# A two-stage expert kernel on one core: moving the first bytes of the streamed tiles from 96 to 48 mod 128

## The chip, the core and the metric

The kernel runs on one core of one Trainium2 chip. The metric is device time in microseconds (us) of one execution; three runs of the kernel before are given, and one further execution was profiled. The engines are TensorE (in the profile PE for matmuls, PEld for the loads of the stationary operand), VectorE (DVE), ScalarE (ACT), GpSimd (POOL) and SyncE (SP, which only issues DMAs here).

## What is computed

The reference takes 8 sequences of 3072 tokens with 256 features and runs three steps, all in float32 accuracy:

```python
X = np.fft.fft(np.fft.fft(x, axis=1), axis=2).real      # 8 x 3072 x 256
x = X.reshape(-1, 256)
h = x @ w_in                                             # 256 -> 2048
x = (h / (1 + np.exp(-1.702 * h))) @ w_out               # 2048 -> 256
e = argmax(x @ w_gate)                                   # of 8 experts, for rows with x @ w_skip > 0
out = x + gate * (relu(x @ w1[e]) @ w2[e])               # 256 -> 1024 -> 256; other rows: out = x
```

## The kernel before

**Numbers.** Every large product is made with operands in the format `fp32r`, each split in a high and a low part, and three matmuls take the place of one: high by high, low by high, high by low. A matmul streams the columns of one operand (the moving tile, 256 columns of 4 bytes in most of them) through 128 columns of the other (the stationary tile), which a LDWEIGHTS loads into the array ahead of it. So each matmul in this kernel has a load of its own, and each load runs beside the matmul before.

**Phase 1** is the class `Phase1`: 16 half-sequences of 768 columns, each in 3 blocks of 256 columns with 8 steps, 384 steps in all. The transform over the tokens is folded into small real matrices `cmat` (L262, 384 columns, 9 matmuls a piece, stationary tiles `sh` and `sl`); its result is written to `yh` and `yl` by ACT, DVE and POOL (`evac_even`, `evac_odd1`, L275 to L296). The transform over the features is folded into the first layer's weights, `wch` and `wcl`. Step g issues, in this order on PE: the first layer (`hstep`, L836, 12 matmuls: `yh` or `yl` streamed, `wch` or `wcl` stationary), then the second layer of step g-2 (`ystep`, L867, 24 matmuls of 264 columns: `woh` or `wol` streamed, `gh` or `gl` stationary), and between them now and then a piece of the next half-sequence's transform or a count for the routing (L779, L781). DVE, ACT and POOL turn a first layer's result into `gh` and `gl` meanwhile.

**Between the phases** (`last_block`) the first blocks of expert 0 are made with the tiles of phase 1: L1030 (`axh` and `axl` streamed, `w1h` and `w1l` stationary, 96 matmuls) and L1065 (`w2h` and `w2l` streamed, `ahh` and `ahl` stationary, 96 matmuls).

**Phase 2** is the class `Phase2`: for each expert, blocks of 256 rows, some of them in a loop whose number of turns comes from the data. A block is `first` (L1253, 48 matmuls: `xh` or `xl` streamed, `w1h` or `w1l` stationary) and `second` (L1289, 48 matmuls: `w2h` or `w2l` streamed, `hh` or `hl` stationary). The 41 blocks of this run give 1968 matmuls on either line. A block's rows are transposed and written to `xh` and `xl` at L1220 and L1221; the next expert's weights are split into `w1h` to `w2l` at L1203 and L1204.

**Where tiles start.** A tile lies at the same bytes of all 128 partitions. The allocator puts each at a multiple of 32 bytes, one after the other, so a small unused tile (`skew`) moves those behind it. In the built program before, the streamed tiles of L836, L1253, L1289 and L1065 start at byte 96 mod 128 and their stationary tiles at byte 32 mod 128. Slices of them lie a multiple of 128 bytes further on, so that this holds for each matmul.

Of the kernel before, what the change touches and what calls it, by code (L numbers as in the profile page):

```python
# [13 lines left out]
F32R = mybir.dt.float32r  # L14
# [9 lines left out]
P = 128  # L24
S = 3072
D = 256
FF = 2048
E = 8
F2 = 1024
# [3 lines left out]
HC = 768  # L33
PB = 256
# [121 lines left out]
def skew(pool, words):  # L156
    pool.tile([P, words], F32, name="skew")


class Phase1:  # L160
    def __init__(self, tc, ctx, nb, a, reg, k):
        self.tc, self.nc, self.nb, self.a, self.reg, self.k = tc, tc.nc, nb, a, reg, k
        self.ident, self.xs = k["ident"], k["xs"]
        self.side = defaultdict(list)
        self.pos = defaultdict(list)
        self.rts = {}
        self.scattered = False
        nc = self.nc
        cp = self.cp = ctx.enter_context(tc.tile_pool(name="cp", bufs=1))
        self.wch = cp.tile([P, 2, FF], F32R, name="wch")  # L170
        self.wcl = cp.tile([P, 2, FF], F32R, name="wcl")
        self.woh = cp.tile([P, NF, NW], F32R, name="woh")
        self.wol = cp.tile([P, NF, NW], F32R, name="wol")
        self.w128 = cp.tile([P, NF], F32, name="w128")
        self.coef = cp.tile([P, 2, CW], F32, name="coef")
        self.spec = cp.tile([P, 4, nb], F32, name="spec")
        self.mini = cp.tile([P, 8], F32, name="mini")
        self.tri = cp.tile([P, 2, P], BF16, name="tri")
        self.rid = cp.tile([P, 2, 4, 2], F32, name="rid")
        self.k8 = cp.tile([P, 4, 8], F32, name="k8")  # L180
        self.base = cp.tile([P, 8], F32, name="base")
        self.base0 = cp.tile([P, 8], F32, name="base0")
        dp = self.dp = ctx.enter_context(tc.tile_pool(name="dp", bufs=1, space=DRAM))
        self.yd = dp.tile([nb, 2, HC], F32, name="yd")
        self.ydm = dp.tile([nb, 1], F32, name="ydm")
        self.ps = ctx.enter_context(tc.tile_pool(name="ps", bufs=1, space=PSUM))
        self.left = ctx.enter_context(ExitStack())
        self.right = ctx.enter_context(ExitStack())
        self.yr = self.open(self.right, "yr", "right")
        self.fa = self.open(self.right, "fa", "right")  # L190
# [105 lines left out]
        le.tensor_sub(dl, xt, dh)  # L296

    def new_y(self, hb):
        pool = self.yl if hb % 2 else self.yr
        return [pool.tile([P, 2, HC], F32R, tag=t, name=t) for t in ("yh", "yl")]  # L300

    def new_s(self):
        sh = self.fa.tile([P, 4, 3, P], F32R, tag="sh", bufs=1, name="sh")
# [30 lines left out]
    def startup(self):  # L334
        nc, a, tc, nb = self.nc, self.a, self.tc, self.nb
        ps = self.ps
        v, act, pool = nc.vector, nc.scalar, nc.gpsimd
# [238 lines left out]
        def close():  # L576
            sts.close()
            self.yl = self.open(self.left, "yl")
            skew(self.yl, 24)
            self.rp = self.open(self.left, "rp")  # L580
            self.fb = self.open(self.right, "fb", "right")
            self.fbufs = 1
# [62 lines left out]
        at(3, "b", load_c, 5)  # L645
        at(4, "b", load_c, 4)
        at(9, "a", close)
        self.cm = cm

# [482 lines left out]
class Phase2:  # L1132
# [25 lines left out]
    def tiles(self):  # L1158
        tc, ctx = self.tc, self.ctx
        cp = self.cp = ctx.enter_context(tc.tile_pool(name="cp2", bufs=1, side="right", reuse_waits="tile"))  # L1160
        self.sp = ctx.enter_context(tc.tile_pool(name="sp2", bufs=2, side="right", reuse_waits="tile"))
        self.xh = cp.tile([P, 2, PB], F32R, name="xh")
        self.xl = cp.tile([P, 2, PB], F32R, name="xl")
        self.cur = cp.tile([P, 2, RW], F32, name="cur")
        skew(cp, 24)
        self.turns, self.t = {}, {}


# [6 lines left out]
    def top(self, e, v=None):  # L1175
        self.t[e] = self.load((self.turns[e] if v is None else v) * PB + e * self.reg, "top", "top")
# [10 lines left out]
        self.r[e] = r1, r2  # L1187

    def weights(self, e):
        shapes = (("w1h", [P, 2, F2]), ("w1l", [P, 2, F2]), ("w2h", [P, E, D]), ("w2l", [P, E, D]))  # L1190
        pool = self.wp[e % 2]
        self.w[e] = [pool.tile(s, F32R, tag=t, name=t) for t, s in shapes[:2]]
        if e < 2:
            skew(pool, 16)
        self.w[e] += [pool.tile(s, F32R, tag=t, name=t) for t, s in shapes[2:]]

    def split(self, e, i):
        r, w = self.r[e], self.w[e]
# [97 lines left out]
    def run(self):  # L1296
        nc, tc = self.nc, self.tc
        self.pool(1)
        self.ps = self.ctx.enter_context(tc.tile_pool(name="ps2", bufs=1, space=PSUM, reuse_waits="tile"))
        hp = self.ctx.enter_context(tc.tile_pool(name="hp2", bufs=1, reuse_waits="tile"))  # L1300
        skew(hp, 16)
        self.hh, self.hl = (hp.tile([P, E, PB], F32R, name=n) for n in ("hh", "hl"))
        w, t, turns, top = self.w, self.t, self.turns, self.top
        top(1)
        self.raws(1, nc.scalar)
        kw = {} if self.sync == "barrier" else dict(iteration_sync=self.sync)
        for e in range(E):
            more = e + 1 < E
            if more and e:
                top(e + 1)  # L1310
            with tc.For_i(0, turns[e], 1, **kw) as i:  # L1311
                nx = self.load(((turns[e] if e else self.v0) - i - 1) * PB + e * self.reg, "nx")
                s, ix = self.first(w[e], {1: self.ready})
                tc.stage_boundary()
                self.transpose(nx)
                self.second(w[e], s, ix, nx, {(0, 2): self.ready, (0, 3): tc.stage_boundary, (0, 5): self.ready, (0, 7): tc.stage_boundary, (1, 4): self.ready})
            if more:
                self.weights(e + 1)

            def mid():  # L1320
                tc.epilogue_barrier()
                if more:
                    tc.prologue_barrier()

            s, ix = self.first(w[e], {j: (lambda j=j: [self.split(e + 1, 2 * j - 2 + z) for z in range(2)]) for j in range(1, 4)} if more else {}, mid)
            if more:
                self.transpose(t[e + 1])
                self.split(e + 1, 6)
                self.split(e + 1, 7)
            if e + 2 < E:  # L1330
                if self.pads is not None:
                    self.pads(e + 2)
                self.raws(e + 2)
            self.second(w[e], s, ix, None)
            if more:
                nc.vector.tensor_copy(self.cur, t[e + 1])
# [49 lines left out]
```

## Time and profile before

| | |
|---|---|
| median of 3 runs | 2401.2 us (2398.43 to 2401.38) |
| profiled execution, its own time | 2397.02 us |
| its span, first to last instruction | 2394.9 us |
| mean granted TensorE clock | 0.997 of 2.4 GHz |
| PE busy | 2341.7 us (98%), 19222 matmuls |
| DVE, ACT, POOL busy | 1652.3 us (69%), 1121.5 us (47%), 1399.2 us (58%) |
| matmuls of L867, L836, L1253, L1289 | 9216, 4608, 1968, 1968 |

The share of a busy PE counts each matmul from its start to a modelled end some 280 ns later, while the next one starts 113 to 125 ns after it. So neither the share nor the mean duration of one matmul tells how fast they follow each other; the start times in the timeline do.

### The profile page before, as it was taken

To read this page: it belongs to the slowest core of one execution; us is meant where nothing else is said; L and a number is where in the kernel's file an instruction comes from. 1 tells how busy PE (TensorE), PEld (TensorE's weight loads), DVE (VectorE), ACT (ScalarE), POOL (GpSimd) and SP (SyncE) were. 2 spreads that over 40 slices of the span, in tenths; PEclk is the share of its full clock that TensorE was granted. 3 is DMA by queue.
4 is the path that set the end of the run, shared out by engine and by line. 5 is a ranking of instruction groups with operands and counts; after the bars stand their busy time and mean duration, and the time that the engine had idled before them with its cause. 6 is when DMAs were issued, how large, how long until landed. Compare 5 with 4: busy or idle time off the path is not lost. (4 is left out here: it accounts for less than half of the span.)

```text
span 2394.9 us, 50491 instructions
## 1 busy us (share of the span) xinstructions
PE 2341.7 (98%) x19222; PEld 2310.1 (96%) x19222; DVE 1652.3 (69%) x3429; ACT 1121.5 (47%) x1451; POOL 1399.2 (58%) x868
## 2 busy tenths in 40 slices
PE   5999999999999999999999999999999999999999
PEld 4899999999999999999999999999999999999999
DVE  7679679767966886697679668965757445555543
ACT  5544545454554554545445544544545333433332
POOL 3567667676677776777767767667666312323211
PEclk9999999999999999999999999999999999999999
DMA  7302311231222113112312221130101312323111
GB/s 263 116 34 78 126 44 66 69 100 41 66 94 68 48 65 118 47 38 86 115 35 79 71 90 48 59 107 21 61 21 33 108 45 85 117 85 119 37 44 40
DMA packets 91450, 178.82 MB, mean 75 GB/s; under 512 B 10896, under 2 KB 66751, under 8 KB 85105
## 3 DMA queue, kind: packets, MB, share of 16 engines
q1 hardware_dynamic: 69488, 96.12, 13.0%
q0 software_dynamic: 20448, 77.87, 9.4%
q8 instruction: 132, 2.16, 0.4%
q10 hardware_dynamic: 1312, 2.10, 0.3%
q14 instruction: 70, 0.57, 0.1%
HBM read 126.21 MB, written 66.59 MB: 81 GB/s over the span
## 5 line engine op out<-in xcount | busy, mean ns | idle before, releaser
L852 POOL TENSOR_TENSOR gl<-h,gh 128x1024 fp32r<-128x1024 f32 x384 | 924.5, 2408 | 510.6 <-ACT h L851 441.9
L850 ACT ACTIVATE gh<-h 128x1024 fp32r<-128x1024 f32 x384 | 407.6, 1061 | 848.1 <-DVE h L843 700.3
L867 PE MATMUL py<-woh,gh 128*128 128x264 f32 x3072 | 773.0, 285 | 2.1 <-ACT rows L873 1.5
L867 PE MATMUL py<-wol,gh 128*128 128x264 f32 x3072 | 770.5, 284 | 0.0
L867 PEld LDWEIGHTS py<-woh,gh 128*128 128x128 f32 x3072 | 578.8, 188 | 4.2 <-ACT rows L873 3.8
L867 PEld LDWEIGHTS py<-wol,gh 128*128 128x128 f32 x3072 | 579.9, 189 | 0.0
L840 DVE SCALAR_TENSOR_TENSOR pp<-rb,w,pt 128x256 f32<-128x256 f32 x768 | 333.3, 475 | 323.0 <-PE pt L836 322.4
L867 PE MATMUL py<-woh,gl 128*128 128x264 f32 x3072 | 459.7, 284 | 0.8 <-POOL gl L852 0.8
L836 PE MATMUL pt<-yh,wch 128*128 128x256 f32 x1536 | 434.3, 283 | 3.2 <-DVE pp L840 2.4
L836 PE MATMUL pt<-yh,wcl 128*128 128x256 f32 x1536 | 429.5, 280 | 1.9 <-DVE wcl L431 1.9
L836 PE MATMUL pt<-yl,wch 128*128 128x256 f32 x1536 | 429.5, 280 | 0.6 <-POOL yl L296 0.4
L851 ACT ACTIVATE h<-h 128x1024 f32<-128x1024 f32 x384 | 407.5, 1061 | 36.2 <-ACT gh L850 1.5
L867 PEld LDWEIGHTS py<-woh,gl 128*128 128x128 f32 x3072 | 408.5, 188 | 1.0 <-POOL gl L852 1.0
L842 DVE TENSOR_TENSOR h<-pp,pt 128x512 f32<-128x512 f32 x384 | 263.9, 687 | 52.7 <-POOL gl L852 1.7
L836 PEld LDWEIGHTS pt<-yh,wch 128*128 128x128 f32 x1536 | 290.9, 189 | 4.4 <-DVE pp L840 3.0
L836 PEld LDWEIGHTS pt<-yl,wch 128*128 128x128 f32 x1536 | 291.1, 190 | 1.0 <-POOL yl L296 0.6
L836 PEld LDWEIGHTS pt<-yh,wcl 128*128 128x128 f32 x1536 | 289.6, 189 | 2.1 <-DVE wcl L431 2.1
L1267 POOL DMA_INDIRECT out<-ob,ix x82 | 80.6, 983 | 338.3 <-DVE ob L1281 336.1
L843 DVE TENSOR_TENSOR h<-pp,pt 128x512 f32<-128x512 f32 x384 | 261.1, 680 | 0.0
L799 POOL DMA_INDIRECT xs<-rows,rix x192 | 194.3, 1012 | 44.0 <-issue 26.0
L1289 PE MATMUL po<-w2h,hh 128*128 128x256 f32 x656 | 189.3, 289 | 0.0
L1253 PE MATMUL h<-xh,w1h 128*128 128x256 f32 x656 | 183.6, 280 | 5.2 <-PEq L1311 4.1
(221 smaller groups left out, 3456.3 us busy)
## 6 DMA issues: line engine op xcount, KB each, us to landing
cmat<-cm POOLq DMA_DIRECT2D x48, 1158.0 KB, 5.6
raw<-raw SPq DMA_DIRECT2D x48, 512.0 KB, 4.8
out<-rows SPq DMA_DIRECT2D x48, 512.0 KB, 2.9
r<-w SPq DMA_DIRECT2D x14, 1024.0 KB, 6.6
nx<-xs SPq DMA_DIRECT2D x33, 266.0 KB, 3.0
rb<-yd SPq DMA_DIRECT2D x48, 128.0 KB, 3.1
wide<-w_in SPq DMA_DIRECT2D x8, 512.0 KB, 8.7
wide<-w_out SPq DMA_DIRECT2D x8, 512.0 KB, 6.1
```

The lines of the kernel that those rows point to most:

```text
L799: i = self.nc.gpsimd.indirect_dma_start(self.xs, bass.IndirectOffsetOnAxis(ap=ix[:, t : t + 1], axis=0), rows[:, t], None, bounds_check=E ...
L836: nc.tensor.matmul(pt[z][:, i], lhsT=w_[:, z, f], rhs=x_[:, z, cols], start=n == 0, stop=n == 2)
L840: v.scalar_tensor_tensor(pp[:, i], r, self.w128[:, 2 * s + i : 2 * s + i + 1], pt[0][:, i], ALU.mult, ALU.add)
L842: v.tensor_add(h[:, :, 0], pp, pt[1])
L843: v.tensor_sub(h[:, :, 1], pp, pt[1])
L850: nc.scalar.activation(gh, hv, AF.Gelu_apprx_sigmoid)
L851: nc.scalar.activation(hv, hv, AF.Gelu_apprx_sigmoid)
L852: nc.gpsimd.tensor_sub(gl, hv, gh)
L867: nc.tensor.matmul(ys[gb][t], lhsT=x_[:, i, tk], rhs=w_[:, 2 * s + i], start=s == 0 and part is hi and n == 0, stop=ends and part is lo an ...
L1253: nc.tensor.matmul(h[:, z], lhsT=w_[:, k, f * P : (f + 1) * P], rhs=x_[:, k], start=i == 0, stop=i == 5)
L1267: d = self.nc.gpsimd.indirect_dma_start(self.out, bass.IndirectOffsetOnAxis(ap=ix, axis=0), ob, None, bounds_check=self.ntok - 1, oob_is_e ...
L1289: self.nc.tensor.matmul(po[t], lhsT=x_[:, f, t * P : (t + 1) * P], rhs=w_[:, f], start=f == 0 and n == 0, stop=f == 7 and n == 2)
```

## The change

All instructions stay, on each engine in their order. What moves is the first byte of some tiles. A helper, `shifted`, takes a tile that is 32 words longer and uses it from a given word on; `yh`, `yl`, `xh`, `xl`, `w2h` and `w2l` are made with it, and the small unused tiles ahead of them go, but for one of expert 0.

```diff
+def shifted(pool, rows, cols, words, name):
+    t = pool.tile([P, rows * cols + 32], F32R, tag=name, name=name)
+    return t[:, words : words + rows * cols].rearrange("p (a b) -> p a b", a=rows)
...
     def new_y(self, hb):
-        pool = self.yl if hb % 2 else self.yr
-        return [pool.tile([P, 2, HC], F32R, tag=t, name=t) for t in ("yh", "yl")]
+        pool, words = (self.yl, 12) if hb % 2 else (self.yr, 20)
+        return [shifted(pool, 2, HC, words, t) for t in ("yh", "yl")]
...
             self.yl = self.open(self.left, "yl")
-            skew(self.yl, 24)
...
-        self.xh = cp.tile([P, 2, PB], F32R, name="xh")
-        self.xl = cp.tile([P, 2, PB], F32R, name="xl")
+        self.xh, self.xl = (shifted(cp, 2, PB, 28, t) for t in ("xh", "xl"))
         self.cur = cp.tile([P, 2, RW], F32, name="cur")
-        skew(cp, 24)
...
     def weights(self, e):
-        shapes = (("w1h", [P, 2, F2]), ("w1l", [P, 2, F2]), ("w2h", [P, E, D]), ("w2l", [P, E, D]))
         pool = self.wp[e % 2]
-        self.w[e] = [pool.tile(s, F32R, tag=t, name=t) for t, s in shapes[:2]]
-        if e < 2:
+        self.w[e] = [pool.tile([P, 2, F2], F32R, tag=t, name=t) for t in ("w1h", "w1l")] + [shifted(pool, E, D, 4, t) for t in ("w2h", "w2l")]
+        if e == 0:
             skew(pool, 16)
-        self.w[e] += [pool.tile(s, F32R, tag=t, name=t) for t, s in shapes[2:]]
...
         hp = self.ctx.enter_context(tc.tile_pool(name="hp2", bufs=1, reuse_waits="tile"))
-        skew(hp, 16)
```

First bytes, mod 128, that the two built programs give the operands of the matmuls (line numbers of the kernel before):

```
line    streamed    before           after     stationary   before   after
L836    yh, yl      96               48        wch, wcl     32       32
L1253   xh, xl      96               48        w1h, w1l     32       32
L1289   w2h, w2l    96               48        hh, hl       32       32
L1065   w2h, w2l    96               48        ahh, ahl     32       32
L1030   axh, axl    32               32        w1h, w1l     32       32
L867    woh, wol    0, 32, 64, 96    same      gh, gl       32       32
L262    cmat        multiples of 8   same      sh, sl       96       96
```

At L867 the first byte goes with the slice: steps with an even number within a block have 0 and 32, those with an odd number 64 and 96. At L262 the rows of `cmat` are 386 words long, so its six slices start at different bytes; the third high slice of every second `cmat` tile starts at byte 48, and where it is the last of its piece, the load beside it is that of the first layer's `wch`, at byte 32.

Beside these, `rows`, `cur` and the tiles of the gate start at other multiples of 32 bytes than before, and one subtraction into `yl` on POOL (L296), early in phase 1, waits for two loads of the startup more than before, since its tile now reaches over another part of the startup's buffers.

## Rows read from the trace of the kernel before

**Rows 1.** The page: the span, and each engine's busy time, share and instructions.
```profile
span 2394.9 us, 50491 instructions
PE 2341.7 (98%) x19222; PEld 2310.1 (96%) x19222; DVE 1652.3 (69%) x3429; ACT 1121.5 (47%) x1451; POOL 1399.2 (58%) x868
```

**Rows 2.** Busy time by stretch, phase 1 and phase 2 (columns in the first line).
```profile
core 0: us, PE busy (x) PEld busy (x) DVE busy (x) ACT busy (x) POOL busy (x), PEclk, DMA share, GB/s
27.90:1858.10 1830.20, 1812.06 (x14808) 1790.37 (x14809) 1370.04 (x2755) 925.53 (x1054) 1256.56 (x712) 1.00 0.21 71
1892.00:2381.00 489.00, 478.52 (x4022) 472.18 (x4022) 241.32 (x557) 176.65 (x363) 118.46 (x110) 1.00 0.26 76
```

**Rows 3.** What PE waited for: us in total, times, longest; the first three.
```profile
PE pmisc L262 <- ACT sh L499: 17.6, 1, 17.6
PE h L1253 <- PEq L1311: 4.1, 7, 2.4
PE pt L836 <- DVE pp L840: 2.4, 2, 2.0
```

**Rows 4.** Timeline of PE, one step: start us, duration, line, tiles.
```profile
410.82 0.28 PE L836 MATMUL pt<-yh,wch 128*128 128x256 f32 x1
410.94 0.28 PE L836 MATMUL pt<-yl,wch 128*128 128x256 f32 x1
411.05 0.28 PE L836 MATMUL pt<-yh,wcl 128*128 128x256 f32 x1
...
412.19 0.28 PE L867 MATMUL py<-woh,gh 128*128 128x264 f32 x1
```

**Rows 5.** The same timeline, the next step and the first start of the one behind it.
```profile
415.10 0.28 PE L836 MATMUL pt<-yh,wch 128*128 128x256 f32 x1
...
416.51 0.29 PE L867 MATMUL py<-woh,gh 128*128 128x264 f32 x1
...
419.42 0.28 PE L836 MATMUL pt<-yh,wch 128*128 128x256 f32 x1
```

**Rows 6.** Timeline of PE, two blocks of phase 2: first and 25th matmul of each.
```profile
1892.15 0.28 PE L1253 MATMUL h<-xh,w1h 128*128 128x256 f32 x1
...
1894.87 0.28 PE L1253 MATMUL h<-xh,w1h 128*128 128x256 f32 x1
...
1907.67 0.28 PE L1253 MATMUL h<-xh,w1h 128*128 128x256 f32 x1
...
1910.49 0.28 PE L1253 MATMUL h<-xh,w1h 128*128 128x256 f32 x1
```

**Rows 7.** Timeline of PE between the phases: first of 12 matmuls, and the one behind.
```profile
1884.70 0.28 PE L1030 MATMUL ah<-axh,w1h 128*128 128x256 f32 x1
...
1886.13 0.28 PE L1065 MATMUL apo<-w2h,ahh 128*128 128x256 f32 x1
```

**Rows 8.** Timeline of PE, the last matmul of two transform pieces, and the one behind.
```profile
320.61 0.33 PE L262 MATMUL pmisc<-cmat,sl 128*128 128x384 f32 x1
320.78 0.28 PE L836 MATMUL pt<-yh,wch 128*128 128x256 f32 x1
...
558.96 0.34 PE L262 MATMUL pmisc<-cmat,sl 128*128 128x384 f32 x1
559.14 0.28 PE L836 MATMUL pt<-yh,wch 128*128 128x256 f32 x1
```

**Rows 9.** Instructions of L836, L1253, L1289: count, duration, first and last start us.
```profile
L836 PE MATMUL pt<-yh,wch x1536: 275/281/561, 27.9 to 1857.8; 128*128 128x256 f32 x192
...
L1253 PE MATMUL h<-xh,w1h x656: 276/280/359, 1892.2 to 2384.1; 128*128 128x256 f32 x164
...
L1289 PE MATMUL po<-w2h,hh x656: 276/280/415, 1900.4 to 2389.5; 128*128 128x256 f32 x164
```

**Rows 10.** Groups of instructions that write the moved tiles: busy, mean ns, idle before.
```profile
L296 POOL TENSOR_TENSOR yl<-xt,yh 128x768 fp32r<-128x768 f32 x16 | 30.1, 1883 | 0.0
L1221 DVE TENSOR_TENSOR xl<-xt,xh 128x512 fp32r<-128x512 f32 x41 | 27.9, 681 | 2.4 <-ACT xh L1220 2.2
```

## The prediction

> **What bounds the kernel now.** I read the page first: PE is busy 98% of the span, the next engine, DVE, 69% [rows 1]. The stretches say that this holds in both phases: in phase 1 DVE is busy 1370 of 1830 us and POOL 1257, in phase 2 no other engine reaches half [rows 2]. The waits say the rest: PE's largest is 17.6 us once at the start, the next 4.1 us over seven times [rows 3]. So PE's own matmuls, one behind the other, set the end, and a nanosecond gained or lost on each of thousands of them arrives nearly whole in the time. The timeline then shows how closely they follow each other, and there the reader is to see something odd. One step of the first layer, 12 matmuls of 256 columns, goes from 410.82 to 412.19, 1.37 us or 114 ns each [rows 4]; the next step, the same instructions on the same tiles, from 415.10 to 416.51, 1.41 us or 118 ns each [rows 5]. In phase 2 a run of 24 takes 2.72 us, 113.3 ns each, and the one a block later 2.82 us, 117.5 ns each [rows 6]. A run is at the one pace or at the other for as long as it lasts; hardly one changes in its middle.
>
> 256 columns at one a cycle of the granted 2.4 GHz are 106.7 ns, so 6.6 ns of each matmul are lost at the quick pace and 11 at the slow one. Nothing in the program differs between two such runs but the moment at which PE comes into them: the quick step takes 0.23 us for its first two (410.82 to 411.05) [rows 4], 115 ns each, before it settles at 113, as if it were pulled into a rhythm, and the slow one never gets there. My reading is that the streamed reads and the reads of the load beside them meet in the memory at some moments, that where they meet goes with the first bytes of the two tiles and with the moment of entry, and that with first bytes 96 and 32 both rhythms keep themselves up. The change moves one of the two first bytes.
>
> **What is touched.** 4608 matmuls of L836, 1968 of L1253, 1968 of L1289 [rows 9] and 96 of L1065. Counting the starts of those lines in the trace between their first and last row [rows 9], and leaving out those with a wait or another line behind them, 4521 of L836 are 116.0 ns apart in the mean, 43% of them 115 or less; 3788 of L1253 and L1289 are 116.5 ns apart, about 30% at the quick pace.
>
> **The unknown price.** No matmul of 256 columns in this trace streams from byte 48 beside a load from byte 32, so its pace has to be bounded. The nearest rows are the last matmuls of some transform pieces, which stream 384 columns from byte 48 while the load of the first layer's stationary tile at byte 32 runs. They are either 170 ns (320.61 to 320.78) or 179 ns (558.96 to 559.14) [rows 8]; of 33 such pairs in the trace 14 are 170, 17 are 179 or 180, two lie between. Per column 170 ns is the quick pace again: 170 times 256 over 384 is 113.3. And 179 is 9 ns worse, twice the step of 4.5 ns between the two paces of today. The lower bound is thus 113.3 for each matmul: 4521 times 2.7 plus 3788 times 3.2 is 24 us gained. The upper bound is 113.3 plus 9, 122.3 for each: 4521 times 6.3 plus 3788 times 5.8, 50 us lost. The other row at hand, 256 columns streamed from byte 32 beside a load from byte 32, takes 1.43 us for 12, 119 ns each [rows 7], and 118.5 in the mean over its 96.
>
> I take a value close to the lower bound. The reason lies in the size of the two steps. A matmul that loses 4.5 ns shifts the entry of the next by a little; today's slow rhythm is one in which such shifts go round without ever hitting the good moment. A matmul that loses 9 ns shifts the next by more, and a sequence that jumps further has fewer ways round a good moment that 14 of 33 entries hit by chance. Once hit, 113.3 keeps itself up, as in the quick runs of today. That is an inference from [rows 8] and [rows 6], not something a row shows.
>
> **The sum.** In L836 a run is 12 long, and a quick one loses some 8 ns as it comes in (0.23 us for its first two, and 1.37 us in all against 12 times 113.3 or 1.36) [rows 4], 0.7 ns on each of 12: 114.0 instead of 116.0, times 4521, is 9.0 us. In L1253 and L1289 the runs are 24 to 48 long and the entry weighs half as much: 113.7 instead of 116.5, times 3788, is 10.6 us. L1065 gives 0.2. Against it stands the second layer, whose 24 matmuls begin at the moment at which the first layer lets go: they took 2.91 us after the quick step (412.19 to 415.10) and 2.91 after the slow one (416.51 to 419.42) [rows 4, 5]. These two steps have other slices of `woh`; comparing like with like over all steps, those with even numbers are 1.2 ns a matmul slower behind a quick step, those with odd numbers 0.1 quicker. 108 even steps would change over, times 24 times 1.2 ns: 3 us given back. In all 9.0 + 10.6 + 0.2 - 3, 17 us less.
>
> **What costs nothing.** The instructions that write the moved tiles are few: 16 of 1.9 us on POOL for a half-sequence's `yl`, 41 of 0.7 us on DVE for a block's `xl` [rows 10]. In phase 1 they lie beside PE, which does not wait for them; with that cover gone the POOL ones would be worth 30 us in all, and a tenth more of it, 3. The `xl` write is on the way from a block's rows to its first product, so a tenth of 28 us, 3 us, is the most it can bring either way. The one longer wait on POOL, ahead of a `yl` subtraction, is for loads of the startup that the startup itself has used; behind it POOL has `gl`, and PE would wait for that, once, for 2 us or so if I am wrong. What is late next once the matmuls are quicker is nothing soon: DVE has 460 us of phase 1 to spare [rows 2].
>
> The profiled execution took 2397.0 us, 4 less than the median of 2401.2, and the sum leaves 2380 of it. Against the median it is 2384, which I predict.
>
> **The rivals.**
>
> *Nothing moves.* The pace is set by the entry alone, and byte 48 has the same two rhythms in about the same shares. For it: 14 and 17 of 33 at byte 48 is a mixture like today's. Against it: 118.5 at L1030 and 116.5 in phase 2 for like instructions say that first bytes count [rows 6, 7]. Time: 2401, give or take 4. The Trainium skill would have it so: TensorE: Matmul & The Clock Gate, Part 2, says that the streamed operand and the weight load have independent read ports into SBUF, and that loading the next weights takes no read bandwidth from the running matmul. By that rule no first byte can matter; this trace speaks against it, with 113.3 and 117.5 ns for the same 24 matmuls.
>
> *Slower.* Byte 48 lies only 16 bytes off the stationary tile's 32, where before it lay 64 off. If what matters is the distance between the two, L1030 with distance 0 is the nearest row, and its pace of 118.5 holds [rows 7]: 4521 times 2.5 plus 3788 times 2.0, 19 us more, 2420. For it: L1030 is the only row with 256 columns at a small distance, and no run of 12 in it settles at 113. It decides as soon as the good moment at byte 48 is too narrow to be hit, that is, as the pace of the affected lines passes 116. In the extreme, with 9 ns lost each time, it is 2451.
>
> *The bytes are not where the title puts them.* The built program has them at 48 and 32 on all four lines, so this is worth 2 in 100, at 2401.
>
> **How the numbers follow.** The forecast has a chance of 0.53, no effect 0.20 with the misplaced bytes, slower 0.27. The forecast's own range is 2373 (the lower bound of 24 us, and no giving back or some gain in the second layer) to 2393 (half the runs still at the slow pace). The range that holds 8 in 10 reaches on through no effect to the slower case as far as 2418, which is a little under its centre; left out are the other half of the slower case and a few in 100 below. 0.2% of the time is 4.8 us, about what a measurement can tell from no change: faster by more 0.54, within it 0.19, slower by more 0.27.
>
> **What will show it.** Right: starts in L836 that settle at 113 to 114 ns in nearly every step, 24 matmuls of L1253 in 2.72 us in nearly every block, L867 between 2.90 and 2.97 us a step, and busy times of DVE, ACT and POOL as before. Wrong: runs of L1253 at 2.82 us or more in most blocks, a pace of 118 or more without a quick one anywhere (the slower case), or a gap before L836 with a releaser on POOL or ACT, which would say that the writes count.

## The result and the profile after

The changed kernel takes 2413.3 us (median of five runs, 2411.0 to 2415.9) against 2401.2 before: 1.0054 times as long, 95% interval 1.0039 to 1.0068. It is slower by 12 us where I forecast 17 less. The profiled execution took 2415.88 us.

I show the same views of it as [rows 1 to 6]. First the page: the span and the busy times (lines of the changed kernel are 4 or 5 higher in phase 1, so L840 is L836 of before and L871 is L867).

```profile
span 2413.9 us, 50492 instructions
PE 2364.8 (98%) x19222; PEld 2334.0 (97%) x19222; DVE 1645.3 (68%) x3429; ACT 1120.7 (46%) x1451; POOL 1395.9 (58%) x868
```

PE has grown by 23 us with the same 19222 matmuls, and DVE, ACT and POOL have not [rows 1]. The view of what PE waited for is as before, too [rows 3]:

```profile
PE pmisc L267 <- ACT sh L504: 17.3, 1, 17.3
PE h L1253 <- PEq L1310: 4.1, 7, 2.3
PE h L1253 <- issue: 2.7, 2, 1.9
PE pt L840 <- DVE pp L844: 2.2, 2, 1.9
```

The third of them was 1.9 us before, and all of PE's waits together are no longer than before. So the time went into the matmuls themselves. The same two steps as in [rows 4, 5], in the timeline of PE:

```profile
414.17 0.28 PE L840 MATMUL pt<-yh,wch 128*128 128x256 f32 x1
...
415.58 0.28 PE L871 MATMUL py<-woh,gh 128*128 128x264 f32 x1
...
418.50 0.28 PE L840 MATMUL pt<-yh,wch 128*128 128x256 f32 x1
...
419.93 0.29 PE L871 MATMUL py<-woh,gh 128*128 128x264 f32 x1
...
422.85 0.28 PE L840 MATMUL pt<-yh,wch 128*128 128x256 f32 x1
```

The two first layers now take 1.41 and 1.43 us, where they took 1.37 and 1.41; the second layer takes 2.92 us twice, where it took 2.91. In phase 2 a run of 24, again by its first and its 25th matmul:

```profile
1920.33 0.28 PE L1253 MATMUL h<-xh,w1h 128*128 128x256 f32 x1
...
1923.15 0.28 PE L1253 MATMUL h<-xh,w1h 128*128 128x256 f32 x1
```

That is 2.82 us. Of 31 such runs in the trace none is shorter, where before 9 of 30 were 2.72 to 2.74 [rows 6]. **The quick pace is gone, and nothing else of that size has happened.** From here on *pace* is the mean time from the start of each matmul of a line to the start of the next matmul on PE, those of 135 ns and more left out, and *quick share* is the part of them of 115 ns or less. Single starts of 115 ns also turn up inside slower rhythms, so a share of up to a quarter or so need not mean more; by *quick rhythm* I mean six or more such starts in a row. In these terms L836, L1253 and L1289 have it before, and no moved line has it after:

| line | before: pace, quick share | after: pace, quick share | all its starts to the next, before and after |
|---|---|---|---|
| L836 | 116.0 ns, 43% | 118.1 ns, 8% | 550.6 to 560.0 us |
| L1253 | 116.6 ns, 28% | 117.9 ns, 6% | 243.1 to 247.0 us |
| L1289 | 116.4 ns, 31% | 117.9 ns, 8% | 240.2 to 242.6 us |
| L867 | 121.9 ns, 0% | 121.8 ns, 0% | 1138.0 to 1137.2 us |

The last column gives 9.4 + 3.9 + 2.4 - 0.8, 15 of the 19 us between the two spans. By paces alone it is 4505 times 2.08 and 3769 times 1.35, 14.5 us, within the interval of the ratio (9 to 16 us). Of the other 4 us, 1.8 lie between the starts of 48 matmuls of 8 columns each (L960), and there the granted clock is at half: the profiled execution has 38.6 us at half clock in all, against 15 before, and this window shows its longest stretch, 10.2 us.

```profile
core 0: us, PE busy (x) PEld busy (x) DVE busy (x) ACT busy (x) POOL busy (x), PEclk, DMA share, GB/s
1773.30:1783.50 10.20, 10.20 (x49) 10.20 (x49) 2.65 (x6) 1.48 (x2) 1.73 (x2) 0.50 0.01 2
```

The granted clock is 0.50 there, the lower level of 1.2 GHz; it falls in the midst of those 48 matmuls. Before, 3.4 us at that place are at half clock. Such stretches differ from kernel to kernel in the experiments too, in no order that I can see, and they are one reason why I judge each experiment by its paces as well as by its time.

### The profile page after: what moved, and what is told of

It is laid out like the page before. It is cut to its first block, busy times and chain, and to the rows that moved or that the text cites. A ratio compares the mean times of both kernels' runs of the same rounds, so it can differ in the third digit from the quotient of the medians.

```text
span 2413.9 us, 50492 instructions
## 1 busy us (share of the span) xinstructions
PE 2364.8 (98%) x19222; PEld 2334.0 (97%) x19222; DVE 1645.3 (68%) x3429; ACT 1120.7 (46%) x1451; POOL 1395.9 (58%) x868
## 5 line engine op out<-in xcount | busy, mean ns | idle before, releaser
L871 PE MATMUL py<-woh,gh 128*128 128x264 f32 x3072 | 774.9, 286 | 1.5 <-ACT rows L877 1.4
L871 PE MATMUL py<-wol,gh 128*128 128x264 f32 x3072 | 773.3, 285 | 0.0
L871 PEld LDWEIGHTS py<-woh,gh 128*128 128x128 f32 x3072 | 580.2, 189 | 3.5 <-ACT rows L877 3.2
L871 PEld LDWEIGHTS py<-wol,gh 128*128 128x128 f32 x3072 | 581.5, 189 | 0.0
L871 PE MATMUL py<-woh,gl 128*128 128x264 f32 x3072 | 459.4, 284 | 0.7 <-POOL gl L856 0.7
L840 PE MATMUL pt<-yh,wch 128*128 128x256 f32 x1536 | 438.2, 285 | 3.1 <-DVE pp L844 2.2
L840 PE MATMUL pt<-yh,wcl 128*128 128x256 f32 x1536 | 433.4, 282 | 0.2 <-DVE wcl L436 0.2
L840 PE MATMUL pt<-yl,wch 128*128 128x256 f32 x1536 | 432.6, 282 | 0.6 <-POOL yl L301 0.4
L871 PEld LDWEIGHTS py<-woh,gl 128*128 128x128 f32 x3072 | 408.6, 188 | 0.9 <-POOL gl L856 0.9
L840 PEld LDWEIGHTS pt<-yh,wch 128*128 128x128 f32 x1536 | 290.8, 189 | 4.3 <-DVE pp L844 2.6
L840 PEld LDWEIGHTS pt<-yl,wch 128*128 128x128 f32 x1536 | 291.0, 189 | 1.0 <-POOL yl L301 0.6
L840 PEld LDWEIGHTS pt<-yh,wcl 128*128 128x128 f32 x1536 | 291.0, 189 | 0.4 <-DVE wcl L436 0.4
L1253 PE MATMUL h<-xh,w1h 128*128 128x256 f32 x656 | 185.6, 283 | 6.0 <-PEq L1310 4.1
L1289 PE MATMUL po<-w2h,hh 128*128 128x256 f32 x656 | 190.4, 290 | 0.0
```

The costliest lines, as they stand in the source:

```text
L840: nc.tensor.matmul(pt[z][:, i], lhsT=w_[:, z, f], rhs=x_[:, z, cols], start=n == 0, stop=n == 2)
L871: nc.tensor.matmul(ys[gb][t], lhsT=x_[:, i, tk], rhs=w_[:, 2 * s + i], start=s == 0 and part is hi and n == 0, stop=ends and part is lo an ...
L1253: nc.tensor.matmul(h[:, z], lhsT=w_[:, k, f * P : (f + 1) * P], rhs=x_[:, k], start=i == 0, stop=i == 5)
L1289: self.nc.tensor.matmul(po[t], lhsT=x_[:, f, t * P : (t + 1) * P], rhs=w_[:, f], start=f == 0 and n == 0, stop=f == 7 and n == 2)
```

## The experiments

**Two things changed, not one.** The diff moves the streamed tile from 64 bytes above its stationary partner to 16 above, mod 128. What I had not read in it: `shifted` makes each tile 128 bytes longer, so that the high and the low part of one operand, which alternate in the stream, start 128 bytes apart mod 256, where before they started at the same byte mod 256. I call the first the distance, the second the gap. All kernels below compute the same; only tiles move. Pairs are written streamed/stationary, first bytes mod 128.

### One phase at a time

Edits against the changed kernel: p1_only puts phase 2 back to byte 96, p2_only phase 1. The longer tiles stay in both.

```diff
p1_only
-        self.xh, self.xl = (shifted(cp, 2, PB, 28, t) for t in ("xh", "xl"))
+        self.xh, self.xl = (shifted(cp, 2, PB, 8, t) for t in ("xh", "xl"))
-  ... [shifted(pool, E, D, 4, t) for t in ("w2h", "w2l")]
+  ... [shifted(pool, E, D, 16, t) for t in ("w2h", "w2l")]
p2_only
-        pool, words = (self.yl, 12) if hb % 2 else (self.yr, 20)
+        pool, words = (self.yl, 24) if hb % 2 else (self.yr, 0)
```

> Only yh and yl start at byte 48; xh, xl, w2h and w2l are back at 96. Pace theory (the start-to-start time of a line goes with the first bytes of its own two tiles, and with nothing else): L836 118.1 ns as in the changed kernel, L1253 and L1289 116.5 as before; 4505 times 2.1 ns, 9.5 us over the kernel before, 2411. Rival (the time came from elsewhere, from stretches at half clock or from tiles that moved along): L836 may be at 118 but the time stays at 2401, or all 12 us are there.

> Only xh, xl, w2h and w2l start at byte 48; yh and yl are back at 96. Pace theory: L836 116.0, L1253 and L1289 117.9; 3770 times 1.35 ns and 0.2 of L1065, 5 us over the kernel before, 2406. Rival (from elsewhere): 2401, or the whole 12 us here.

p1_only: 2411.6 us, 1.0038 (1.0026 to 1.0051). p2_only: 2407.6 us, 1.0026 (1.0016 to 1.0036). The half that stays at byte 48 does what was expected: L836 goes at 118.1 ns in p1_only, L1253 and L1289 at 117.9 in p2_only. The surprise lies in the half that was put back. In p1_only phase 2 is at 96/32 as before, yet L1253 goes at 117.8 and L1289 at 117.7 ns; in p2_only L836 is at 96/32 and goes at 117.6. So byte 48 cannot be all of it.

### The gap alone

gap96 is the kernel before, all bytes 96/32, with 128 unused bytes between the high and the low tile of `y`, `x` and `w2`.

```diff
+def apart(pool, shape, hi, lo, first):
+    h = pool.tile(shape, F32R, tag=hi, name=hi)
+    if first:
+        pool.tile([P, 32], F32, name="gap")
+    return [h, pool.tile(shape, F32R, tag=lo, name=lo)]
```

> The kernel before with 128 unused bytes between the high and the low tile of each pair (yh and yl, xh and xl, w2h and w2l); all streamed rows still start at byte 96 mod 128. New theory (the pace goes with how a matmul's streamed row lies to that of the matmul before it, and the change put high and low tiles 128 bytes mod 256 apart, by the 128 bytes that each tile is longer): L836 117.6 ns and L1253 117.8, as in p2_only and p1_only at byte 96; 4521 times 1.6 plus 3788 times 1.3, 12 us more than before, 2414. First-byte theory: 116.0 and 116.5, 2402.

2410.5 us, 1.0028 (1.0016 to 1.0040); L836 117.5, L1253 117.8, L1289 117.6 ns. The run of 24 in its timeline:

```profile
1917.39 0.28 PE L1259 MATMUL h<-xh,w1h 128*128 128x256 f32 x1
...
1920.22 0.28 PE L1259 MATMUL h<-xh,w1h 128*128 128x256 f32 x1
```

2.83 us, and 11 of its 31 runs round to 2.82, 20 to 2.83. Unused bytes between two tiles take the quick rhythm away, with every first byte mod 128 as before. None of the six kernels with a gap of 128 (this one, the changed one, p1_only, p2_only, m32_all and d64_phase2) has it in L836, L1253, L1289 or L1065.

### Byte 48 alone

c48 has the change's 48/32 with no gap: high and low part lie in one tile, one behind the other.

```diff
+def pair(pool, rows, cols, words, name, gap=0):
+    n = rows * cols
+    t = pool.tile([P, 2 * n + 32 + gap], F32R, tag=name, name=name)
+    return [t[:, w : w + n].rearrange("p (a b) -> p a b", a=rows) for w in (words, words + n + gap)]
...
+        return pair(pool, 2, HC, words, "y")
...
+        self.xh, self.xl = pair(cp, 2, PB, 28, "x")
```

> All moved tiles start at byte 48 as in the changed kernel, but high and low lie in one tile, one right behind the other, so that both have the same byte mod 256. New theory: the two paces of 113.3 and some 118 come back, 116 in the mean or less, 2401 or less; if byte 48 lets the quick pace in more often, as I predicted of the change, nearly all at 113.3 to 114, 2385. First-byte theory: 118 on all lines as in the changed kernel, 2413.

2415.0 us, 1.0052 (1.0035 to 1.0069); L836 118.7, L1253 118.7, L1289 118.0 ns.

```profile
1931.50 0.40 PE L1259 MATMUL h<-x,w1h 128*128 128x256 f32 x2
...
1934.35 0.40 PE L1259 MATMUL h<-x,w1h 128*128 128x256 f32 x2
```

24 matmuls in 2.85 us (the profile joins two neighbours into a row; its first number is the start of the first). So L836, L1253 and L1289 lose the rhythm at 48/32 without any gap, and either of the two things is enough by itself.

### Other distances

m32_all puts everything at 32/32 with the change's gap; d64_phase2 has 112/48 in phase 2, distance 64 again, and 16/32 and 80/32 in the even and odd half-sequences of phase 1, all with the gap; cA and cB spread other distances over the lines, without gap. Of their edits one line each, against the changed kernel and against c48:

```diff
m32_all
+        self.xh, self.xl = (shifted(cp, 2, PB, 24, t) for t in ("xh", "xl"))
d64_phase2
+        self.hh, self.hl = (shifted(hp, E, PB, 4, n) for n in ("hh", "hl"))
cA
+        self.xh, self.xl = pair(cp, 2, PB, 16, "x")
cB
+        self.xh, self.xl = pair(cp, 2, PB, 4, "x")
```

> All the moved tiles start at byte 32, like their stationary tiles, distance 0. Theory that the distance between the two first bytes counts and a small one is bad: 118.5 ns or more on L836, L1253 and L1289 as on L1030, 2416 to 2420. Theory that a row that begins off a multiple of 32 bytes is what costs: 116 as at byte 96, 2401.

> Phase 2 keeps the old distance of 64 bytes with both sides 16 bytes further: xh, xl, w2h, w2l at 112, w1h, w1l, hh, hl at 48. Distance theory: 116.5 ns on L1253 and L1289 with quick runs at 113 among them, as before. Theory of the 16 bytes off the grid of 32: 118 there. In phase 1 even half-sequences stream from byte 16 and odd ones from 80 (distance 112 and 48): the distance theory has the first near 118.5 and the second nearer 116; the other has both at 118.

> High and low in one tile as in c48, other first bytes: even half-sequences 64, odd ones 80, x 0, w2 of even experts 112 and of odd ones 16. A look for a first byte at which the quick pace of 113.3 is kept throughout. New theory without a role for the first byte: about 116 on each. With a role for the distance to byte 32: best near 64 bytes of distance (byte 80 to 112), worst near 0 (byte 16).

> As cA with even half-sequences 112, odd ones 16, x 80, w2 of even experts 64 and of odd ones 0. Same question: the same byte should give the same pace in L836, L1253 and L1289, as far as the byte decides.

One run each, 2411.2, 2410.0, 2419.6 and 2414.4 us. m32_all: L836 117.9, L1253 118.5, L1289 118.4 ns. cA, with 0/32 at L1253: 119.8; L836 with 64/32 and 80/32 in the even and odd half-sequences: 118.0 and 119.0. cB, with 80/32 at L1253: 118.4; L836 with 112/32 in the even half-sequences: 118.9. d64_phase2 has L1253 at 117.6 and L1289 at 117.4 ns with a quarter of the starts quick, but no quick rhythm, where before they went at 116.6 and 116.4: the right distance with the gap does not do it.

**One pair does not fit.** The odd half-sequences of cB are at 16/32, 16 bytes from the partner as in the change, but on its other side. They have the quick rhythm: 117.1 ns, 34% quick, and 32 of the 162 steps without a wait take 1.36 us. One of them, from its first start to that of the line behind it:

```profile
424.66 0.39 PE L846 MATMUL pt<-y,wch 128*128 128x256 f32 x2
...
426.02 0.28 PE L877 MATMUL py<-woh,gh 128*128 128x264 f32 x1
```

Its expectation had small distances as the worst. L1289, at 16/32 for every second expert in cA, does not have the rhythm.

### Distance 64 without the gap, at other bytes

D_dist64 has 112/48 in phase 2 without gap, 96/32 in the even half-sequences of phase 1 and 24/32 in the odd ones. E_gap256 keeps 96/32 at L1253 with a gap of 256 bytes, and puts the other lines a few bytes off: 88/32 and 104/32 at L836, 92/32 and 100/32 at L1289.

```diff
D_dist64, against c48
+        pool, words = (self.yl, 6) if hb % 2 else (self.yr, 0)
+        self.xh, self.xl = pair(cp, 2, PB, 12, "x")
+        self.w[e] = pair(pool, 2, F2, 4, "w1") + pair(pool, E, D, 20, "w2")
+        self.hh, self.hl = pair(hp, E, PB, 4, "hh")
E_gap256, against c48
+        pool, words = (self.yl, 26) if hb % 2 else (self.yr, 30)
+        self.xh, self.xl = pair(cp, 2, PB, 8, "x", 64)
+  ... pair(pool, E, D, 17 if e % 2 else 15, "w2")
```

> Each pair of high and low tile in one tile, with no gap. Phase 2 at the old distance of 64 bytes with both sides 16 further: streamed rows at 112, stationary tiles at 48. Distance theory (streamed minus stationary byte decides, 64 is the good one): L1253 and L1289 at two paces of 113.3 and some 118 again, 116.5 in the mean. Byte theory (the streamed row's own byte decides, 96 is the good one): 118 or more, as at byte 112 beside 32. Phase 1, even half-sequences at 96: 116.0 as in the kernel before, else the one tile for both has an effect of its own. Odd ones at 24: a look, no theory.

> Streamed rows of L1253 at byte 96 with 256 unused bytes between high and low tile. Theory that the gap of 128 matters as half of 256: back to 116.5 and the two paces, as without a gap. Theory that any gap disturbs: 117.8 as with 128. The other tiles look around byte 96, without gaps: even half-sequences 88, odd ones 104, w2 of even experts 92 and of odd ones 100. If the good place is a narrow one at 64 bytes of distance, these stay at 117 to 119; if it is wide, some are at 116 or below.

One run each again. D_dist64: L1253 at 114.8 ns with 72% quick, L1289 at 114.9 with 71%; of its 30 runs of 24, 22 take 2.72 to 2.73 us. Two of its blocks, joined into one row each:

```profile
1920.82 3.34 PE L1259 MATMUL h<-x,w 128*128 128x256 f32 x28
...
1955.46 3.36 PE L1259 MATMUL h<-x,w 128*128 128x256 f32 x27
```

Less the last one's 0.28, that is 3.06 us over 27 steps, 113.3 ns, and 3.08 over 26, 118.5 ns. A rhythm at both paces again, with neither 96 nor 32 in it. Its time, 2408.5 us, is no better than before for the sake of phase 1: 24/32 costs 120.6 ns, and the even half-sequences, at 96/32 without gap, hardly ever got into the rhythm (117.7 ns, 5% quick, 7 of 164 steps), which the prediction's own argument of the entry allows and I had not expected.

E_gap256 has both paces at L1253 as well, 116.0 ns and 42%, 16 of 33 runs in 2.73 us and 17 in 2.83:

```profile
2090.63 0.40 PE L1259 MATMUL h<-x,w1h 128*128 128x256 f32 x2
...
2093.46 0.40 PE L1259 MATMUL h<-x,w1h 128*128 128x256 f32 x2
...
2102.69 0.40 PE L1259 MATMUL h<-x,w1h 128*128 128x256 f32 x2
...
2105.42 0.39 PE L1259 MATMUL h<-x,w1h 128*128 128x256 f32 x2
```

A gap of 256 is as good as none; a gap of 128 is not. The lines that are 4 or 8 bytes off distance 64 went at 120.1 and 120.2 ns, slower than at any pair of multiples of 16, and the time was 2413.4 us.

### Phase 2 at four pairs of distance 64

Phase 1 is exactly that of the kernel before. In phase 2 high and low part lie in one tile, and only the words differ; here those of F_phase2_112_48 and J_phase2_48_112.

```diff
F_phase2_112_48
+        self.xh, self.xl = pair(cp, 2, PB, 12, "x")
+        self.w[e] = pair(pool, 2, F2, 4, "w1") + pair(pool, E, D, 20, "w2")
+        self.hh, self.hl = pair(hp, E, PB, 4, "hh")
J_phase2_48_112
+        self.xh, self.xl = pair(cp, 2, PB, 28, "x")
+        self.w[e] = pair(pool, 2, F2, 20, "w1") + pair(pool, E, D, 4, "w2")
+        self.hh, self.hl = pair(hp, E, PB, 20, "hh")
```

> Phase 1 as in the kernel before (96 beside 32, tiles as they were). In phase 2 all four lines of tiles start 16 bytes further, 112 streamed beside 48 stationary, high and low rows 0 apart mod 256. Distance theory (64 bytes between the two, high and low alike mod 256, gives the quick rhythm; the bytes themselves do not matter): L836 at 116.0 ns as before, L1253 and L1289 at about 114.8 ns with 70% of the starts at 115 or less, which is 3770 times 1.75, 6.6 us less than before: 2395, ratio 0.9973. Rival one (with the right distance the share of quick runs is set by the moment of entry alone, which D_dist64 met better by chance): 116.5 ns in both lines and 2401. Rival two (96 and 32 themselves are the good bytes): L1253 near 118 and 2407.

> As F_phase2_112_48 (high and low parts of phase 2 in one tile each, phase 1 as before), but at the bytes of the kernel before: 96 streamed beside 32 stationary. If the bytes 112 and 48 gave the larger share of quick runs: L1253 and L1289 at 116.5 ns and about 30% as before, 2401. If one tile for both parts, or the moment at which PE enters, gave it: 115 ns and 65%, 2396. In neither case may the quick rhythm be gone (117.8).

> As F_phase2_112_48, with 80 streamed beside 16 stationary, distance 64 again. Distance theory: the quick rhythm is there, L1253 and L1289 between 114.5 and 116.5 ns with 30% or more of the starts at 115 or less, 2393 to 2401. If only some bytes at distance 64 are good: 117.8 and none locked, 2407.

> As F_phase2_112_48 with the two bytes exchanged: streamed at 48, the byte of the change, beside stationary at 112; the streamed tile lies 64 below its partner, which is 64 above mod 128. Distance theory mod 128: byte 48 is as good as any, the quick rhythm is there, 114.5 to 116.5 ns, 2393 to 2401. If 64 above and 64 below differ (a period of more than 128 bytes), or if byte 48 itself is bad: 117.8 or more, 2407 to 2410.

| kernel | phase 2 | L836 | L1253, quick | L1289, quick | time | ratio to before |
|---|---|---|---|---|---|---|
| H | 96/32 | 116.0 ns | 116.9 ns, 21% | 116.4 ns, 32% | 2400.8 us | 0.9995 (0.9985 to 1.0005) |
| I | 80/16 | 116.0 | 115.1, 65% | 115.2, 64% | 2397.8 | 0.9983 (0.9973 to 0.9993) |
| F | 112/48 | 116.0 | 115.1, 66% | 115.1, 65% | 2396.5 | 0.9974 (0.9964 to 0.9984) |
| J | 48/112 | 116.0 | 114.2, 84% | 115.6, 55% | 2394.7 | 0.9965 (0.9954 to 0.9975) |

This is the decisive set. **J streams from byte 48, as the change does, and has the lowest time of the study** (its interval overlaps those of F and I), quicker than both kernels compared: byte 48 is not bad, 16 bytes above its partner is. L836, untouched, stays at 116.0 in all four. H says that one tile for both parts gives nothing by itself: at the old bytes the old paces and the old time come back. So in these two lines the distance of 64 lets the quick rhythm in, and the bytes, or the moments of entry that go with them, decide how often it is met. A block of J in the timeline of PE, 26 steps in 2.95 us:

```profile
1910.96 3.23 PE L1260 MATMUL h<-x,w 128*128 128x256 f32 x27
```

### The first layer at other pairs of distance 64

G has 112/48 in both phases; K and L have J's phase 2 and in phase 1 48/112 and 80/16. `wch` and `wcl` are moved for that.

```diff
G_112_48_both
+        self.wch, self.wcl = pair(cp, 2, FF, 4, "wc")
+        pool, words = (self.yl, 28) if hb % 2 else (self.yr, 4)
K_48_112_both
+        self.wch, self.wcl = pair(cp, 2, FF, 20, "wc")
+        pool, words = (self.yl, 12) if hb % 2 else (self.yr, 20)
L_80_16_phase1
+        self.wch, self.wcl = pair(cp, 2, FF, 28, "wc")
+        pool, words = (self.yl, 20) if hb % 2 else (self.yr, 28)
```

> 112 streamed beside 48 stationary in both phases, high and low rows 0 apart mod 256; the second layer's tiles and the transform as before. Distance theory: no line loses the quick rhythm; L836 between 113.6 (every run locked) and 117.7 (none, as in the even half-sequences of D_dist64), by the moment of entry, L1253 and L1289 near 114.8: 2390 to 2404. Byte theory (96 and 32 are the good bytes in the first layer): L836 at 118, two ns more on 4500, with L1253 and L1289 no better than 116.5: 2410.

> As J_phase2_48_112, with the first layer too at 48 streamed beside 112 stationary. Distance theory: L836 keeps the quick rhythm (114 to 116.5 ns, 40% or more of the starts at 115 or less), L1253 and L1289 as in J_phase2_48_112. Time 2385 to 2397 if PE's other waits stay as in the kernel before; up to 15 us more if, as in G_112_48_both, a VectorE instruction of every second half-sequence falls behind GpSimd's gl and PE waits for it. If the first layer's gain is bound to 96 and 32: L836 at 118 and 2404.

> As J_phase2_48_112, with the first layer at 80 streamed beside 16 stationary. Distance theory: as for K_48_112_both, L836 between 114 and 116.5 ns with 40% or more quick, 2385 to 2397, or up to 15 us more with a VectorE instruction behind gl in every second half-sequence. If the first layer's gain is bound to 96 and 32: L836 at 118 and 2404.

L836 in G: 116.3 ns, 46% quick. In K: 116.3 ns and 43% in the odd half-sequences, 118.4 and none in the even ones. In L: 116.0 and 48% odd, 117.1 and 24% even. The quick rhythm is thus there at each of the three pairs, and hardly more often met than before. K takes 2400.6 us and L 2399.6, both 0.9986 (0.9976 to 0.9995), which is less gain than J has alone. Both miss what was expected, 2385 to 2397 us, and K's even half-sequences, at distance 64 without a gap, have no quick rhythm at all.

G was a miss of another kind. L836 is at its pace of before within 0.3 ns, L867 within 0.1, L1253 and L1289 are quicker, and it takes 2411.9 us, 1.0036 (1.0023 to 1.0049). In its view of PE's waits these three have grown, from 0.8, 2.4 [rows 3] and 0.3 us:

```profile
PE py L876 <- POOL gl L861: 5.0, 7, 0.8
PE pt L845 <- DVE pp L849: 3.9, 8, 2.0
...
PE pmisc L788 <- DVE roh L779: 3.3, 6, 0.6
```

They recur in every second half-sequence. The timeline of DVE and of POOL ahead of one such place:

```profile
401.63 2.48 DVE L241 TENSOR_TENSOR va<-eo 64x128 f32<-64x128 f32 x1
```

```profile
401.57 2.38 POOL L861 TENSOR_TENSOR gl<-h,gh 128x1024 fp32r<-128x1024 f32 x1 [1.21 <-ACT h L860]
```

And the same two instructions in the kernel before:

```profile
399.06 0.29 DVE L231 TENSOR_TENSOR va<-eo 64x128 f32<-64x128 f32 x1
```

```profile
399.09 2.54 POOL L852 TENSOR_TENSOR gl<-h,gh 128x1024 fp32r<-128x1024 f32 x1 [1.28 <-ACT h L851]
```

Before, the VectorE subtraction starts 0.03 us ahead of POOL's and takes 0.29 us. In G it starts 0.06 us behind it, and takes 2.48 us, until just behind the end of POOL's. Six of the 16 instructions of that line take 2.47 or 2.48 us, where before the longest is 0.33. DVE has hardly a gap in the following steps, so PE waits there for `pp`, `gl` and `roh`, and the half-sequence pair comes out at 224.5 instead of 222.3 us. H and F have one such subtraction each, of 2.54 us, in one pair of half-sequences, and that pair alone is longer, in H 224.5 instead of 222.3; K and L have none. That of H starts 0.01 us behind POOL's:

```profile
624.27 2.54 DVE L242 TENSOR_TENSOR va<-eo 64x128 f32<-64x128 f32 x1
```

```profile
624.26 2.40 POOL L863 TENSOR_TENSOR gl<-h,gh 128x1024 fp32r<-128x1024 f32 x1 [1.25 <-ACT h L862]
```

Trainium Architecture — The Big Picture, a page of the Trainium skill, has under "What this means for kernel authors" that VectorE and GpSimd contend for a shared port pair, as an exclusive lock and not a split of bandwidth. The rows of G and H fit that. The same sentence says that within the engine side only this pair contends; whether what L836 and L1253 do with their first bytes is contention at all, no run here shows.

## Why the prediction was wrong

*What bounds the kernel: right.* PE's own matmuls set the end, PE's waits together did not grow, and the paces arrived nearly whole: 14.5 us by paces, 12 measured.

*Two paces, chosen by the entry, with first bytes at work in them: right.* But the entry is not chance, as the prediction had it. Of the eight steps in a block of phase 1, numbered from 0, those with numbers 1 and 5 all end quick in the trace before (93 of 93 without a wait, the last four starts 114.5 ns apart or less in the mean), and of those with 2 and 7 one of 93. The Trainium skill's rule of independent read ports (TensorE: Matmul & The Clock Gate, Part 2), which the prediction set against it, would have left the time at 2401; F, H, I and J alone, with the same instructions, differ by 6 us, and the changed kernel by 12.

*What costs nothing: right.* The writers of the moved tiles take what they took (1876 and 680 ns in the mean, 1883 and 681 before); DVE and POOL are busy 7 and 3 us less than before, not more.

*The terms of the sum:*

| term | forecast | measured in the trace after |
|---|---|---|
| L836 | -9.0 us | +9.4 us (118.1 ns, not 114.0) |
| L1253 and L1289 | -10.6 us | +6.4 us (117.9 ns, not 113.7) |
| L1065 | -0.2 us | +0.2 us (92 times 118.0 less 115.7) |
| L867 | +3 us | -0.8 us |

The 1.2 ns behind the 3 us of L867 do not come out of the trace: over the even steps with nothing in between it is 0.6 ns (122.5 behind a quick step, 121.9 behind a slow one), and at the two places in a block where both occur 0.2 more and 0.3 less.

**The step that failed** is "I take a value close to the lower bound", with its reason that "a sequence that jumps further has fewer ways round a good moment" and that "once hit, 113.3 keeps itself up". The rows behind it were single intervals of 170 ns [rows 8]: one matmul, followed by one of another line and length. They show that two neighbours can be 113.3 ns apart per 256 columns at 48/32, and not that the next two will be. In c48 single starts of 115 ns turn up in every block of L1253, between others of 117 to 122, and pull nothing in: no six in a row in L836, L1253 or L1289, and the pace is 118.7. The rhythm can keep itself up at 48/32, but it is hardly ever hit: without a gap L1065 has it in one of its eight runs of 12, in c48 as in K and L (in J in none), where before, at 96/32, it has it in four. Six of these matmuls in c48, 0.68 us or 113.3 ns each:

```profile
1883.22 0.39 PE L1075 MATMUL apo<-w,ahh 128*128 128x256 f32 x2
...
1883.90 0.39 PE L1075 MATMUL apo<-w,ahh 128*128 128x256 f32 x2
```

In the changed kernel, with the gap, not even L1065 has it. The bounds themselves held: 117.9 and 118.1 lie between 113.3 and 122.3.

*The rival "Slower" was the right mechanism.* It named the distance, with L1030 at distance 0 as its row [rows 7], and put the point of decision at 116 ns. The runs bear it out, J most of all, but for 16/32 in cB. Its price was too high: L1030's 118.5 ns taken for 48/32 gave 19 us, where 118.1 and 117.9 were measured, and 12 to 15 us.

*What I did not see in the diff* is the gap. It is in the two lines of `shifted`, 32 words more for each tile. Alone it costs 7 us by gap96's ratio (4 to 10), more than half of the result; with distance 16 it adds next to nothing (c48 1.0052, the change 1.0054), since the rhythm can be lost only once. I had counted it as bytes that nobody reads.

**What stays open.** For these tiles no kernel with a gap of 128 mod 256 has the quick rhythm in a moved line, and with a gap of 0 or 256 all four pairs at distance 64 mod 128 have it. But distance 64 is not enough, as K's even half-sequences show, nor is it strictly needed, as 16/32 in cB and L1065 at 48/32 show; why 16 below its partner should be better than 16 above is open. Which resource the stream and the load share, if they do, was not tried. Nor is it settled what sets the share of quick runs: 21% at 96/32, 66% at 112/48 and 84% at 48/112 in L1253 look regular (G and D, both 112/48, have 63% and 72%; K and L, both 48/112, 79% and 82%), but at 96/32 it is 28% before and 42% in E_gap256, and in phase 1 even and odd half-sequences of one kernel differ as much.

## What to carry to other kernels

Where each matmul has a load of its own, the first byte of a streamed tile means nothing without that of its stationary partner: here 64 bytes apart mod 128 allowed 113.3 ns in most places, and 16 above it, 0 or a few bytes off 64 cost 118 to 120. Count the bytes of padding too, since they move every tile behind them against its partners and its twin. And before a rate is taken for a steady one, look for several in a row: one quick interval says that it can happen, a run of them that it stays.

## What the hardware showed beside this

The steady rhythms are not of any length. By start times over long runs, the quick one is 113.33 ns a matmul, 17 times 6.667 ns; the slow one of 96/32 repeats 117, 118, 118 ns, 353.3 for three or 53 times 6.667; and L1030's repeats after five, 593.3, or 89 times 6.667. And tiles that start 8 bytes off a multiple of 16 (88, 104 and 24 against 32) gave 120.1 to 120.6 ns, worse than every multiple of 16 tried in L836; 92 and 100, 4 bytes off, did the same in L1289. No row here says why.
